# Attention and a two-layer projection on one core: where the second part of batch 0 runs, when w_out is requested, who builds the masks, and which PSUM banks the first projection uses

## The chip, the core and the metric

The kernel runs on one core of a Trainium2 chip. The metric is device time in microseconds (us), the median of several executions of the same program. The profile is of one execution; its span of 255.1 us is a little shorter than the measured time, 256.92 us.

Five engines work side by side, each through its own list of instructions in order: TensorE (PE, matmuls and transposes), VectorE (DVE), ScalarE (ACT), GpSimd (POOL) and SyncE (SP, which here only requests transfers). DMA engines move data between HBM and the core's memory.

## The reference

For 4 batches, 8 heads, 768 positions and 64 numbers per head, attention with one of two masks, then a projection to 2048, a leaky ReLU with a slope per column, and a projection back to 512:

```python
scores = scale * q @ k.T                      # per batch and head, 768 x 768
causal = rel >= 0                             # rel = row - column
stream_keep = causal & (is_sink | in_win)     # first 4 columns, and a window of 64
mask = causal if is_retrieval[h] else stream_keep   # heads 0, 2 and 6 are retrieval heads
a = softmax(where(mask, scores, -1e9))
x = (a @ v), heads side by side               # 3072 tokens x 512
h = x @ w_in                                  # 3072 x 2048
g = maximum(h, 0) + alpha * minimum(h, 0)
out = g @ w_out                               # 3072 x 512, float32
```

## The kernel before

**Segments.** Attention is cut into segments, each of one batch and one pair of heads. Batch 0 is cut in two: segments 0 to 3 ("a") are its first 512 positions, segments 4 to 7 ("b") the other 256. Segments 8 to 19 are batches 1 to 3, whole. A segment runs through pieces: `S` (scores on TensorE, exp on ScalarE, a mask multiplied in on VectorE for segments from 4 on), `AV` (weighted values on TensorE, division on VectorE), and `X` (transposes on TensorE, copy to `xT` on VectorE). `Tq` and `Tk` transpose q and k of the next segment; from segment 12 on a transfer transposes them instead.

**Projections.** Tokens are cut into eight tiles: tile 2b is the first 512 positions of batch b, tile 2b+1 its other 256. `P1(t, f)` computes 128 of the 2048 columns of the first projection for tile t: four matmuls into one PSUM bank, then `neg` (ScalarE, L489) and `g` (VectorE, L490), which frees the bank. `P2(t, s, quarter)` is a quarter, four matmuls, of the second projection for 128 tokens; after four quarters ScalarE copies the result out and a transfer writes it.

**Order of the work.** The order is written out by hand and kept as written (`manual_schedule`). `pieces` lists the attention of segments 4 to 19 in order; `plan` lists units of P1 and P2 to be put between them, spread evenly by cost (a P2 quarter or a 512-wide P1 unit counts 1, a 256-wide P1 unit 0.5). Each entry of `plan` holds the units that run until the last segment of a batch (or of batch 0's second part) is nearly finished; what is left is put there at once, and the next entry begins. After the last piece comes the tail, projections only.

**Before the woven part.** After segments 0 to 3, P1 of tile 0 runs alone for `f` 0 to 12: first three of the four matmuls of units 0 to 4 (the lead), X(3), their fourth matmuls, then units 5 to 12 on up to eight banks. Between these units VectorE builds the multiplicative masks `mr`, `ms` and `ms5` from the additive ones `nmr` and `nms`. Only then do segments 4 to 7 begin, with P1 units 13 to 15 and the first eight units of P2(0) between their pieces.

**Buffers and queues.** Loaded float32 q, k and v rest in `qf`, `kf` and `vf`, four of each in turn. Casts to bf16 are `cast` on GpSimd for segments 0 to 7 (L178 to L199) and `whole_q`, `whole_k`, `whole_v` on VectorE for segments 8 to 19 (L205, L214 or L218, L228), called one or two segments ahead: `whole_q(9)` comes before the first piece of segment 8, `whole_k(9)` before its third, `whole_v(9)` before its fifth. With segment 8 the fifth piece is X(7), the last of batch 0. Loads of q, k and v are requested on SyncE (queue q1 in the profile); `w_in` (three transfers) and `w_out` (four) on GpSimd (q0)[...]. `w_out` is requested right behind `w_in` and the casts of segment 3, ahead of the loads of segments 4 to 11. The memsets of `vf`, `kf`, `kT` and `natk` on GpSimd stand between.

**PSUM.** Of eight banks, `sc0` and `sc1` hold scores, `m0` to `m2` transposes and `AV` results (from segment 4 on `m0` and `m1` only), `mm2` and `m2` P2 results, and P1 takes `mm0` and `mm1`, or the first `wide` names of

```python
WIDE = ["mm0", "mm1", "sc0", "sc1", "mm2", "m0", "m1", "m2"]
```

Of the kernel before, what the change touches and what calls it, by code (L numbers as in the profile page):

```python
# [9 lines left out]
ALU = mybir.AluOpType  # L10
# [4 lines left out]
def kernel(  # L15
# [13 lines left out]
    nc = tc.nc  # L29
    B, H, S, D = q.shape  # L30
# [4 lines left out]
    fp32 = DT.float32  # L35
# [4 lines left out]
    NSINK = 4  # L40
# [5 lines left out]
    CROSS = 12  # L46
# [31 lines left out]
    NSEG = len(SEGS)  # L78
# [5 lines left out]
    ps = ctx.enter_context(tc.tile_pool(name="ps", bufs=1, space=bass.MemoryType.PSUM))  # L84
# [3 lines left out]
    NF, NK, NV, NR, NS = 4, 5, 6, 2, 3  # L88
    qf = [stat.tile([128, 2, 6, 64], fp32, name=f"qf{i}") for i in range(NF)]
    kf = [stat.tile([128, 7, 2, 64], fp32, name=f"kf{i}") for i in range(NF)]  # L90
    vf = [stat.tile([128, 7, 2, 64], fp32, name=f"vf{i}") for i in range(NF)]
# [4 lines left out]
    kT_all = stat.tile([128, NK, 2, 7 * 128], bf16, name="kT")  # L96
# [9 lines left out]
    NATK = [stat.tile([128, 2 * 960], bf16, name=f"natk{i}") for i in range(2)]  # L106
# [14 lines left out]
    def load(n):  # L121
        load_qk(n, nc.sync)
        load_rows(n, v, vf)
# [25 lines left out]
    def ka(n):  # L149
        T = (SEGS[n].q1 - SEGS[n].q0) // 128  # L150
        flat = kf[n % NF].rearrange("p i h d -> p (i h d)")
        return flat[:, 0:2 * T * 64].rearrange("p (h i d) -> p h i d", h=2, d=64)
# [14 lines left out]
    natq, natk = {}, {}  # L167
# [34 lines left out]
    def whole_q(n):  # L202
        sg = SEGS[n]
        nat = natq[n] = NATQ[n % 2]
        nc.vector.tensor_copy(nat.rearrange("p i (h d) -> p h i d", h=2), qf[n % NF])  # L205
        if n >= CROSS:
            nc.sync.dma_start(qT[sg.seq % NK][:, 0:S].rearrange("p (i r) -> p i r", r=128),
                              nat.rearrange("p i c -> p (i c)"), transpose=True)

    def whole_k(n):  # L210
        sg = SEGS[n]
        if n < CROSS:
            natk[n] = NATK1[n % 2]
            nc.vector.tensor_copy(natk[n].rearrange("p i (h d) -> p h i d", h=2), ka(n))  # L214
            return
        flat = NATK[n % 2]
        rows = flat.rearrange("p (h x) -> p h x", h=2)[:, :, 0:896].rearrange("p h (t c) -> p h t c", c=128)
        nc.vector.tensor_copy(rows[:, :, :, 0:D], kf[n % NF].rearrange("p t h d -> p h t d"))  # L218
        sinks(n, rows)
        for hh, h in enumerate(sg.heads):  # L220
            nt = 6 if RETR[h] else 7
            nc.sync.dma_start(kTs[sg.seq % NK][hh][:, 0:128 * nt].rearrange("p (i r) -> p i r", r=128),
                              flat[:, 896 * hh:896 * hh + 128 * nt], transpose=True)

    def whole_v(n):
        sg = SEGS[n]
        vv = vb[sg.seq % NV]
        nc.vector.tensor_copy(vv[:, :, :, 0:D], vf[n % NF])  # L228
        sinks(n, vv.rearrange("p t h c -> p h t c"))

    load_qk(0, nc.scalar)
# [15 lines left out]
    mr = const.tile([128, 5, 144], bf16, name="mr")  # L247
    ms = const.tile([128, 2, 192], bf16, name="ms")
    ms5 = const.tile([128, 2, 192], bf16, name="ms5")
    nmr = const.tile([128, 5, 144], bf16, name="nmr")  # L250
    nms = const.tile([128, 192], bf16, name="nms")
# [35 lines left out]
    def load_w_out(n):  # L287
        nc.gpsimd.dma_start(w_out_b[:, 4 * n:4 * n + 4, :],
                            moe_w_out[512 * n:512 * (n + 1), :].rearrange("(a p) f -> p a f", p=128))
# [175 lines left out]
    TOK = [(b * S + o, w) for b in range(B) for o, w in ((0, SPLIT), (SPLIT, S - SPLIT))]  # L465
    n_mm = [0]


    WIDE = ["mm0", "mm1", "sc0", "sc1", "mm2", "m0", "m1", "m2"]

    def mm_bank(wide=0):
        n_mm[0] += 1
        return ps.tile([128, 512], fp32, tag=WIDE[n_mm[0] % (wide or 2)], name="mm")

    half_done = {}

    def P1(t, f, cs=range(4), wide=0):
        o, w = TOK[t]
        o %= 2 * S
        psg = half_done.pop((t, f)) if (t, f) in half_done else mm_bank(wide)  # L480
        for c in cs:
            a = PAIRS[c][0] // 2
            nc.tensor.matmul(psg[:, 0:w], w_in_b[:, a, 128 * f:128 * (f + 1)], xT[:, c, o:o + w],  # L483
                             start=(c == 0), stop=(c == 3))
        if cs[-1] < 3:
            half_done[t, f] = psg
            return
        neg = work.tile([128, 512], fp32, tag="neg", name="neg", bufs=3)
        nc.scalar.activation(neg[:, 0:w], psg[:, 0:w], AF.Relu, scale=-1.0)  # L489
        nc.vector.scalar_tensor_tensor(g_buf[t % 2][:, f, 0:w], neg[:, 0:w], oma[:, f:f + 1], psg[:, 0:w],  # L490
                                       op0=ALU.mult, op1=ALU.add)
# [16 lines left out]

            (nc.gpsimd if t < 6 else nc.sync).dma_start(out[r:r + 128, :], ot)  # L509

    def p1_units(t, fs=range(16), wide=0):
        return [(TOK[t][1] / 512, lambda f=f: P1(t, f, wide=wide)) for f in fs]

    def p2_units(t):
        return [(1, lambda s=s, u=u: P2(t, s, u)) for s in range(TOK[t][1] // 128) for u in range(4)]
# [33 lines left out]
    for lo, hi in ((0, 512), (512, 1024), (1024, 2048)):  # L549
        load_w_in(lo, hi)  # L550
    cast_v(3)
    for i in range(4):
        load_w_out(i)
    for i in range(NF):
        nc.gpsimd.memset(vf[i][:, 6, :, :], 0.0)
        nc.gpsimd.memset(kf[i][:, 6, :, :], 0.0)
    nc.gpsimd.memset(kT_all[:, 4].bitcast(fp32), 0.0)
    for nat in NATK:
        nc.gpsimd.memset(nat.bitcast(fp32), 0.0)
    for n in range(4, 8):  # L560
        load(n)
        cast(n)
    for n in range(8, 8 + NF):
        load(n)
    for n in range(4):
        sa, sb = seg_scores(n)
        first = [lambda: AV(n - 1, 1)] if n else []
        if n < 3:
            first += [lambda: Tq(n + 1), lambda: Tk(n + 1)]
        seq = sa[:2] + first + sa[2:] + sb[:1]  # L570
        seq += ([lambda: X(n - 1)] if n else []) + sb[1:] + [lambda: AV(n, 0)]
        for piece in seq:
            piece()
        if n == 2:

            tra = ps.tile([128, 16], fp32, tag=misc_tag(), name="tra")
            nc.tensor.transpose(tra, alpha_r, ident_f)
            nc.vector.tensor_scalar(oma, tra, -1.0, 1.0, op0=ALU.mult, op1=ALU.add)
    AV(3, 1)
    LEAD = 5  # L580
    n_misc[1] = 2
    n_mm[0] = -1
    for f in range(LEAD):
        P1(0, f, range(3), wide=5)
    X(3)
    for f in range(LEAD):
        P1(0, f, range(3, 4))
    n_mm[0] = 4
    for f in range(LEAD, 8):
        P1(0, f, wide=8)  # L590
    n_mm[0] = -1
    for f in range(8, 13):
        P1(0, f, wide=5)
        if f == 8:
            nc.vector.tensor_scalar(mr, nmr, 0.0, None, op0=ALU.is_equal)
        elif f < 11:
            nc.vector.tensor_scalar(ms[:, f - 9, :], nms, 0.0, None, op0=ALU.is_equal)
        elif f == 11:

            nc.vector.tensor_copy(ms5[:, 0, :], ms[:, 0, :])  # L600
            nc.vector.tensor_copy(ms5[:, 1, 0:148], ms[:, 0, 0:148])
        else:
            nc.vector.tensor_copy(ms5[:, 1, 148:192], ms[:, 0, 0:44])
            nc.vector.memset(ms5[0:NSINK, 1, 148:152], 0.0)


    pieces = [([], lambda: Tq(4), []), ([], lambda: Tk(4), [])]
    for n in range(4, NSEG):
        seq, x_at = seg_pieces(n)
        for i, piece in enumerate(seq):  # L610
            pre = []
            if i in (0, 2, 4):
                fn = (whole_q, whole_k, whole_v)[i // 2]
                pre = [lambda m=m, fn=fn: fn(m) for m, lo, hi in ((n + 1, 8, CROSS), (n + 2, CROSS, NSEG)) if lo <= m < hi]
            if i == 4 and 8 <= n < NSEG - NF:
                pre.append(lambda n=n: load(n + NF))
            ready = []
            if x_at and i == x_at - 1 and (n - 1) % 4 == 3:
                b = (n - 1) // 4 - 1
                ready = [1] if b == 0 else [2 * b, 2 * b + 1]  # L620
            pieces.append((pre, piece, ready))
# [4 lines left out]
    def merge(a, z):  # L626

        keyed = [((i + 0.5) / len(x), n, u) for n, x in enumerate((a, z)) for i, u in enumerate(x)]
        return [u for _, _, u in sorted(keyed, key=lambda k: k[:2])]


    second = [p2_units(t) for t in range(8)]
    plan = [p1_units(0, range(13, 16)) + second[0][:8],
            merge(second[0][8:], p1_units(1)) + second[1][:6],
            second[1][6:] + p1_units(2) + merge(second[2], p1_units(3)) + second[3][:6],
            second[3][6:] + p1_units(4) + merge(second[4], p1_units(5)) + second[5][:6]]
    units, budget = plan.pop(0), 0
    for i, (pre, piece, ready) in enumerate(pieces):
        for f in pre:
# [9 lines left out]
        while units and budget >= units[0][0] / 2:  # L649
            c, u = units.pop(0)  # L650
            budget -= c
            u()
    n_mm[0] = -1
    for _, u in second[5][6:] + p1_units(6, wide=4) + merge(second[6], p1_units(7, wide=4)) + second[7]:
        u()
    return nc

# [34 lines left out]
```

## Time and profile before

| what | value |
|---|---|
| time, median of 3 runs | 256.92 us (256.82 to 257.19) |
| span of the profiled run | 255.1 us |
| busy: PE, DVE, ACT, POOL | 236.5, 176.3, 143.7, 46.7 us |
| P1 matmuls (L483) | 512, 100.3 us busy |
| P2 matmuls (L502) | 384, 96.9 us busy |
| `neg` (L489), `g` (L490) | 128 each; 491 and 612 ns mean |
| read from HBM, written to HBM | 27.46 MB, 6.29 MB |

The stages on the profile's clock: segments 0 to 3 until about 20.3 us; P1(0) alone until 33.4; segments 4 to 7 until about 58; batch 1 until 97; batch 2 until 153.8; batch 3 until 209.8; the tail until 251.4, after which the last results are written out. A busy time counts an instruction from its start to its end, and neighbouring instructions on one engine overlap by some tens of ns, so sums of durations run a little over the wall time.

### The profile page before, as it was taken

To read this page: it belongs to the slowest core of one execution; us is meant where nothing else is said; L and a number is where in the kernel's file an instruction comes from. 1 tells how busy PE (TensorE), PEld (TensorE's weight loads), DVE (VectorE), ACT (ScalarE), POOL (GpSimd) and SP (SyncE) were. 2 spreads that over 40 slices of the span, in tenths; PEclk is the share of its full clock that TensorE was granted. 3 is DMA by queue.
4 is the path that set the end of the run, shared out by engine and by line. 5 is a ranking of instruction groups with operands and counts; after the bars stand their busy time and mean duration, and the time that the engine had idled before them with its cause. 6 is when DMAs were issued, how large, how long until landed. Compare 5 with 4: busy or idle time off the path is not lost.

```text
span 255.1 us, 5559 instructions
## 1 busy us (share of the span) xinstructions
PE 236.5 (93%) x2079; PEld 145.2 (57%) x2079; DVE 176.3 (69%) x454; ACT 143.7 (56%) x308; POOL 46.7 (18%) x112
## 2 busy tenths in 40 slices
PE   7898988788889999989999999989999999999994
PEld 6784454546676665445666655446666654456651
DVE  6783998786989995897767755887556537853320
ACT  5871884546676556675555537666555426743320
POOL 7899223101012121010111120010000000000000
PEclk9999999999999999999999999999999999999999
DMA  7999999999995999989395992050111111002112
GB/s 213 281 167 210 206 208 234 213 234 229 205 250 104 243 181 240 208 132 191 83 222 136 177 215 88 8 99 1 44 41 41 44 41 44 0 0 84 44 42 82
DMA packets 94563, 34.96 MB, mean 137 GB/s; under 512 B 84920, under 2 KB 92104, under 8 KB 94536
## 3 DMA queue, kind: packets, MB, share of 16 engines
q1 hardware_dynamic: 88824, 25.16, 50.9%
q0 software_dynamic: 5136, 8.91, 14.9%
q10 hardware_dynamic: 576, 0.53, 0.6%
q8 instruction: 16, 0.26, 0.5%
q14 instruction: 11, 0.09, 0.1%
HBM read 27.46 MB, written 6.29 MB: 132 GB/s over the span
## 4 chain that ended last, share of the span: by engine, by line
PE 61%; DVE 16%; DMA 11%; ACT 5%; issue 3%; POOL 1%; SPq 1%; ACTq 0%; DVEq 0%
PE po L502 28%; PE mm L483 22%; DVE g L490 6%; DMA w_in_b<-in_moe_w_in_dram 5%; PE pav L445 4%; ACT neg L489 3%; PE sc L382 2%; DMA vf<-in_v_dram 2%; DMA kf<-in_k_dram 2%; PE sc L414 2%; DMA qf<-in_q_dram 2%; PE tr L460 2%; DVE xn L452 2%; DVE eS L426 1%; DVE kT L327 1%
## 5 line engine op out<-in xcount | busy, mean ns | idle before, releaser
L483 PE MATMUL mm<-xT,w_in_b 128*128 128x512 bf16 (+1 forms) x512 | 100.3, 326 | 4.8 <-DVE g L490 3.0
L490 DVE SCALAR_TENSOR_TENSOR g<-neg,oma,mm 128x512 bf16<-128x512 f32 (+1 forms) x128 | 77.7, 612 | 36.2 <-ACT neg L489 33.6
L502 PE MATMUL po<-w_out_b,g 128*128 128x512 bf16 x384 | 96.9, 379 | 0.0
L489 ACT ACTIVATE neg<-mm 128x512 f32<-128x512 f32 (+1 forms) x128 | 62.5, 491 | 50.5 <-PE mm L483 49.6
L483 PEld LDWEIGHTS <-w_in_b 128*128 128x128 bf16 x512 | 47.9, 97 | 39.4 <-issue 7.0
L502 PEld LDWEIGHTS <-g 128*128 128x128 bf16 x384 | 35.5, 97 | 27.2
L389 ACT ACTIVATE eR<-sc 128x455 bf16<-128x455 f32 (+5 forms) x72 | 38.6, 553 | 16.1 <-PE sc L382 14.6
L421 ACT ACTIVATE eS<-sc 128x384 bf16<-128x384 f32 x60 | 29.2, 490 | 15.5 <-PE sc L414 13.3
L382 PE MATMUL sc<-qT,kT 128*128 128x268 bf16 (+16 forms) x141 | 24.9, 263 | 1.5 <-DVE kT L336 0.8
L506 ACT COPY ot<-po 128x512 f32<-128x512 f32 x24 | 14.0, 585 | 19.7 <-PE po L502 19.7
L509 POOL DMA_DIRECT2D out_dram<-ot x18 | 9.8, 543 | 83.8 <-ACT ot L506 72.5
L426 DVE TENSOR_TENSOR eS<-eS,ms 128x384 bf16<-128x384 bf16 x50 | 17.9, 360 | 7.2 <-ACT eS L421 7.0
L452 DVE TENSOR_TENSOR xn<-pav,rcp 128x448 bf16<-128x448 f32 (+2 forms) x40 | 21.8, 545 | 1.4
L414 PE MATMUL sc<-qT,kT 128*128 128x192 bf16 (+4 forms) x150 | 21.1, 231 | 0.4 <-ACT eR L389 0.3
L392 DVE TENSOR_TENSOR eR<-eR,mr 128x128 bf16<-128x128 bf16 (+4 forms) x60 | 12.8, 232 | 10.7 <-ACT eR L389 10.4
L382 PEld LDWEIGHTS <-kT 128*128 128x128 bf16 x141 | 11.9, 97 | 10.8 <-DVE kT L336 1.9
L414 PEld LDWEIGHTS <-kT 128*128 128x128 bf16 x150 | 13.6, 98 | 5.7
L445 PE MATMUL pav<-vb,eS 128*128 128x65 bf16 x270 | 13.4, 194 | 3.5 <-DVE eS L426 1.9
L445 PEld LDWEIGHTS <-eS 128*128 128x128 bf16 x270 | 11.3, 97 | 7.9 <-DVE eS L426 2.5
L445 PEld LDWEIGHTS <-eR 128*128 128x128 bf16 x336 | 11.8, 97 | 2.5
L462 DVE COPY xT<-tr 128x768 bf16<-128x768 bf16 (+2 forms) x20 | 9.5, 473 | 5.2 <-PE tr L460 5.2
L445 PE MATMUL pav<-vb,eR 128*128 128x65 bf16 x336 | 12.7, 193 | 0.0
(78 smaller groups left out, 154.4 us busy)
## 6 DMA issues: line engine op xcount, KB each, us to landing
qf<-in_q_dram SPq DMA_DIRECT2D x12, 384.0 KB
vf<-in_v_dram SPq DMA_DIRECT2D x24, 192.0 KB
out_dram<-ot POOLq DMA_DIRECT2D x18, 256.0 KB, 3.4
kf<-in_k_dram SPq DMA_DIRECT2D x16, 192.0 KB
w_out_b<-in_moe_w_out_dram POOLq DMA_DIRECT2D x4, 512.0 KB, 18.5
kf<-in_k_dram SPq DMA_DIRECT2D x4, 384.0 KB
out_dram<-ot SPq DMA_DIRECT2D x6, 256.0 KB
qf<-in_q_dram SPq DMA_DIRECT2D x4, 256.0 KB
```

What stands on the lines that cost most here:

```text
L382: nc.tensor.matmul(sc[:, a - lo:z - lo], kt[:, 128 * j:128 * (j + 1)], qt[:, c:c + z - a], start=True, stop=not masked)
L389: nc.scalar.activation(e[:, lo:hi], sc[:, 0:hi - lo], AF.Exp, scale=scale)
L414: nc.tensor.matmul(sc[:, o:o + z - a], kt[:, 128 * j:128 * (j + 1)], qt[:, 124 * j + a:124 * j + z], start=True, stop=not on_pe)
L421: nc.scalar.activation(two, sc[:, 0:384].rearrange("p (s c) -> p s c", c=192), AF.Exp, scale=scale)
L426: nc.vector.tensor_tensor(two, two, ms5 if first == 4 else ms, op=ALU.mult)
L445: nc.tensor.matmul(pav[:, i, :], e[:, o:o + 128], vv[:, j, hh, 0:D + 1], start=(m == 0), stop=(m == len(terms) - 1))
L452: nc.vector.tensor_tensor(xn[n][:, lo:hi, 64 * hh:64 * hh + 64], pav[:, lo:hi, 0:D], rcp[:, lo:hi].to_broadcast([128, hi - lo, D]), op=ALU ...
L483: nc.tensor.matmul(psg[:, 0:w], w_in_b[:, a, 128 * f:128 * (f + 1)], xT[:, c, o:o + w], start=(c == 0), stop=(c == 3))
L489: nc.scalar.activation(neg[:, 0:w], psg[:, 0:w], AF.Relu, scale=-1.0)
L490: nc.vector.scalar_tensor_tensor(g_buf[t % 2][:, f, 0:w], neg[:, 0:w], oma[:, f:f + 1], psg[:, 0:w], op0=ALU.mult, op1=ALU.add)
L502: nc.tensor.matmul(po[t], g_buf[t % 2][:, f, 128 * s:128 * (s + 1)], w_out_b[:, f, :], start=(f == 0), stop=(f == 15))
L506: nc.scalar.copy(ot, po.pop(t))
```

## The change

The first projection of tile 0 no longer runs alone. After its lead of five units, segments 4 to 7 begin at once, and units 5 to 15 are put between their pieces, on four banks (`mm0`, `mm1`, `mm2`, `m2`), which are free for them because no P2 unit runs there any more. All of P2(0) moves behind X(7), into batch 1, and the later entries of the plan are shifted to suit: P1 of an even tile is now merged with the rest of the P2 before it, not put behind it. In the tail, P2(5) is merged with P1(6).

To let segments 4 to 8 start early, their loads go ahead of `w_out`, which GpSimd now requests behind its casts of q and k of segment 8. Those casts, and that of v, move from VectorE to GpSimd; the casts of q of segments 9 to 11 move to ScalarE. The masks are built on GpSimd, before the loads of segments 4 to 7 come in, since segment 4 needs them earlier and VectorE is busy then.

```diff
-        nc.vector.tensor_copy(nat.rearrange("p i (h d) -> p h i d", h=2), qf[n % NF])
+        copy = nc.gpsimd.tensor_copy if n == 8 else nc.scalar.copy if n < CROSS else nc.vector.tensor_copy
+        copy(nat.rearrange("p i (h d) -> p h i d", h=2), qf[n % NF])
...
-            nc.vector.tensor_copy(natk[n].rearrange("p i (h d) -> p h i d", h=2), ka(n))
+            (nc.gpsimd if n == 8 else nc.vector).tensor_copy(natk[n].rearrange("p i (h d) -> p h i d", h=2), ka(n))
...
-        nc.vector.tensor_copy(vv[:, :, :, 0:D], vf[n % NF])
+        (nc.gpsimd if n == 8 else nc.vector).tensor_copy(vv[:, :, :, 0:D], vf[n % NF])
...
+    BANKS = {"beside P2": ["mm0", "mm1"], "beside attention": ["mm0", "mm1", "mm2", "m2"],
+             "lead": ["mm0", "mm1", "sc0", "sc1", "mm2"], "tail": ["mm0", "mm1", "sc0", "sc1"]}
...
     cast_v(3)
-    for i in range(4):
-        load_w_out(i)
+
+    nc.gpsimd.tensor_scalar(mr, nmr, 0.0, None, op0=ALU.is_equal)
+    for i in range(2):
+        nc.gpsimd.tensor_scalar(ms[:, i, :], nms, 0.0, None, op0=ALU.is_equal)
+    nc.gpsimd.tensor_copy(ms5[:, 0, :], ms[:, 0, :])
+    nc.gpsimd.tensor_copy(ms5[:, 1, 0:148], ms[:, 0, 0:148])
+    nc.gpsimd.tensor_copy(ms5[:, 1, 148:192], ms[:, 0, 0:44])
+    nc.gpsimd.memset(ms5[0:NSINK, 1, 148:152], 0.0)
     for i in range(NF):
         nc.gpsimd.memset(vf[i][:, 6, :, :], 0.0)
-        nc.gpsimd.memset(kf[i][:, 6, :, :], 0.0)
-    nc.gpsimd.memset(kT_all[:, 4].bitcast(fp32), 0.0)
-    for nat in NATK:
-        nc.gpsimd.memset(nat.bitcast(fp32), 0.0)
     for n in range(4, 8):
         load(n)
         cast(n)
-    for n in range(8, 8 + NF):
+    for i in range(NF):
+        nc.gpsimd.memset(kf[i][:, 6, :, :], 0.0)
+    nc.gpsimd.memset(kT_all[:, 4].bitcast(fp32), 0.0)
+    load(8)
+    whole_q(8)
+    whole_k(8)
+    for i in range(4):
+        load_w_out(i)
+    whole_v(8)
+    for n in range(9, 8 + NF):
         load(n)
+    for nat in NATK:
+        nc.gpsimd.memset(nat.bitcast(fp32), 0.0)
...
-    n_mm[0] = 4
-    for f in range(LEAD, 8):
-        P1(0, f, wide=8)
     n_mm[0] = -1
-    for f in range(8, 13):
-        P1(0, f, wide=5)
-        if f == 8:
-            nc.vector.tensor_scalar(mr, nmr, 0.0, None, op0=ALU.is_equal)
...
-    plan = [p1_units(0, range(13, 16)) + second[0][:8],
-            merge(second[0][8:], p1_units(1)) + second[1][:6],
-            second[1][6:] + p1_units(2) + merge(second[2], p1_units(3)) + second[3][:6],
-            second[3][6:] + p1_units(4) + merge(second[4], p1_units(5)) + second[5][:6]]
+    hidden = [p1_units(t) for t in range(6)]
+    plan = [p1_units(0, range(LEAD, 16), "beside attention"),
+            hidden[1][:6] + merge(second[0], hidden[1][6:]) + second[1][:4],
+            merge(second[1][4:], hidden[2]) + merge(second[2], hidden[3]) + second[3][:2],
+            merge(second[3][2:], hidden[4]) + merge(second[4], hidden[5]) + second[5][:2]]
...
-    for _, u in second[5][6:] + p1_units(6, wide=4) + merge(second[6], p1_units(7, wide=4)) + second[7]:
+    for _, u in merge(second[5][2:], p1_units(6, where="tail")) + merge(second[6], p1_units(7, where="tail")) + second[7]:
         u()
```

More of the change, by code (lines that the diff above doesn't have):

```diff
@@ L466, with mm_bank, P1 @@
     n_mm = [0]
-    WIDE = ["mm0", "mm1", "sc0", "sc1", "mm2", "m0", "m1", "m2"]
-    def mm_bank(wide=0):
+    BANKS = {"beside P2": ["mm0", "mm1"], "beside attention": ["mm0", "mm1", "mm2", "m2"],
+             "lead": ["mm0", "mm1", "sc0", "sc1", "mm2"], "tail": ["mm0", "mm1", "sc0", "sc1"]}
+    def mm_bank(where):
         n_mm[0] += 1
-        return ps.tile([128, 512], fp32, tag=WIDE[n_mm[0] % (wide or 2)], name="mm")
+        return ps.tile([128, 512], fp32, tag=BANKS[where][n_mm[0] % len(BANKS[where])], name="mm")
     half_done = {}
-    def P1(t, f, cs=range(4), wide=0):
+    def P1(t, f, cs=range(4), where="beside P2"):
         o, w = TOK[t]
         o %= 2 * S
-        psg = half_done.pop((t, f)) if (t, f) in half_done else mm_bank(wide)
+        psg = half_done.pop((t, f)) if (t, f) in half_done else mm_bank(where)
         for c in cs:
@@ L509, in P2, with p1_units @@
             (nc.gpsimd if t < 6 else nc.sync).dma_start(out[r:r + 128, :], ot)
-    def p1_units(t, fs=range(16), wide=0):
-        return [(TOK[t][1] / 512, lambda f=f: P1(t, f, wide=wide)) for f in fs]
+    def p1_units(t, fs=range(16), where="beside P2"):
+        return [(TOK[t][1] / 512, lambda f=f: P1(t, f, where=where)) for f in fs]
     def p2_units(t):
@@ L583 @@
     for f in range(LEAD):
-        P1(0, f, range(3), wide=5)
+        P1(0, f, range(3), where="lead")
     X(3)
@@ L587 @@
         P1(0, f, range(3, 4))
-    n_mm[0] = 4
-    for f in range(LEAD, 8):
-        P1(0, f, wide=8)
     n_mm[0] = -1
-    for f in range(8, 13):
-        P1(0, f, wide=5)
-        if f == 8:
-            nc.vector.tensor_scalar(mr, nmr, 0.0, None, op0=ALU.is_equal)
[L596 to L604, printed above, removed]
     pieces = [([], lambda: Tq(4), []), ([], lambda: Tk(4), [])]
@@ L613 @@
                 fn = (whole_q, whole_k, whole_v)[i // 2]
-                pre = [lambda m=m, fn=fn: fn(m) for m, lo, hi in ((n + 1, 8, CROSS), (n + 2, CROSS, NSEG)) if lo <= m < hi]
+                pre = [lambda m=m, fn=fn: fn(m) for m, lo, hi in ((n + 1, 9, CROSS), (n + 2, CROSS, NSEG)) if lo <= m < hi]
             if i == 4 and 8 <= n < NSEG - NF:
```

## The prediction

> **What bounds the kernel now.** I read the page's engine shares first: TensorE is busy in 93% of the span, yet a busy share cannot say whether it is running or waiting inside a pipeline. So I took the start of every matmul from TensorE's timeline and gave each the spacing it has where nothing stands in front: 0.216 us for 512 columns (64 in 13.81 us in the chain of waits below), in proportion for fewer, 0.030 us for 65 columns (27 in 0.81 us), 0.056 us for a transpose (six from 52.63 to 52.97). Wall minus this work is stall. The stages come from the windows view (start:end, length, busy us of each engine, clock, DMA share, GB/s):
>
> ```profile
> 20.30:33.40 13.10, 12.19 (x65) 5.42 (x64) 8.91 (x17) 6.84 (x12) 6.86 (x21) 1.00 1.18 208
> 33.40:58.40 25.00, 19.99 (x217) 12.20 (x215) 21.34 (x77) 14.52 (x33) 5.24 (x16) 1.00 1.14 221
> 58.40:97.20 38.80, 36.67 (x408) 25.84 (x408) 33.30 (x99) 24.62 (x57) 5.57 (x13) 1.00 1.00 205
> 97.20:119.00 21.80, 20.14 (x164) 10.63 (x163) 17.37 (x37) 15.05 (x29) 1.79 (x5) 1.00 1.12 188
> 119.00:153.80 34.80, 34.80 (x305) 22.25 (x303) 23.76 (x61) 18.13 (x43) 5.01 (x11) 1.00 0.87 170
> 153.80:175.00 21.20, 19.59 (x139) 10.02 (x137) 16.58 (x36) 14.82 (x29) 1.79 (x5) 1.00 0.22 49
> 175.00:209.80 34.80, 34.70 (x323) 22.31 (x321) 19.46 (x50) 16.14 (x39) 2.70 (x5) 1.00 0.10 39
> 209.80:251.40 41.60, 41.52 (x225) 21.71 (x222) 19.64 (x32) 18.85 (x39) 0.54 (x1) 1.00 0.10 39
> ```
>
> Stall by my count, stage by stage: 1.6 (first projection alone), 7.4 (second part of batch 0), 4.2 (batch 1), 3.3 (P1 of tile 2 beside batch 2), 0.5, 3.3 (P1 of tile 4 beside batch 3), 0.8, 0.65 (tail). TensorE's work is the same in both kernels, so only these 22 us can be won, and any delay adds. After 58.4 us they sum to 12.8.
>
> In the two 3.3 us stages the chain of waits (start, length, what) shows why: with two banks, P1 waits for ScalarE's `neg`, then VectorE's `g`, 2.4 us per two units.
>
> ```profile
> 102.26 0.61 ACT neg L489
> 102.86 0.03 issue
> 102.89 0.76 DVE g L490
> 103.65 0.04 issue
> 103.69 1.04 PE mm L483 x4
> ...
> 209.81 13.81 PE mm L483 x64
> ```
>
> From 20 to 58 us the DMA engines are full as well. The DMA view of 25 to 40 us (queue: packets, MB, share) shows the weights' queue q0 taking three times what q1, with q, k and v, gets; meanwhile GpSimd's timeline shows casts of segment 5 waiting for loads:
>
> ```profile
> q0 software_dynamic: 2122, 2.30, 88.8%
> q1 hardware_dynamic: 2118, 0.79, 30.7%
> ...
> 28.77 0.40 POOL L178 CAST g<-qf 128x256 bf16<-128x256 f32 x1 [2.46 <-DMA qf<-in_q_dram]
> 30.66 0.40 POOL L178 CAST g<-kf 128x256 bf16<-128x256 f32 x1 [1.50 <-DMA kf<-in_k_dram]
> ```
>
> The end of batch 0 is this stretch of VectorE's timeline; the last row is what the first P1 of tile 1 waits for:
>
> ```profile
> 56.97 0.55 DVE L214 CAST natm<-kf 128x768 bf16<-128x768 f32 x1
> ...
> 57.57 0.62 DVE L228 CAST vb<-vf 128x896 bf16<-128x896 f32 x1
> 58.10 0.28 DVE L462 COPY xT<-tr 128x256 bf16<-128x256 bf16 x1
> ```
>
> `whole_k(9)` and `whole_v(9)` stand ahead of it in VectorE's order, in both kernels. Adding up q1's packets in order of end puts q, k and v of segment 9 at about 49, 51 and 53 us: four to six us of slack, no more.
>
> [...]
>
> **The change part by part.**
> *P1(0) units 5 to 12 leave the stage 20.3:33.4* and go beside segments 4 to 7. The lead (20 matmuls, 4.3 us, with X(3)'s wait) ends at about 25.3, so `Tq(4)` comes some 8 us sooner. Those segments keep eleven filler units (before 3 of P1 and 8 of P2; now 11 of P1). Each P1 in place of a P2 adds 0.6 us ScalarE and about 0.67 us VectorE (0.75 less the overlap with its neighbour): 8 x 0.67 = 5.4 us more on VectorE.
> *Four banks* for these units: they remove a wait that would otherwise be the 2.4 us per two units above; price nothing.
> *Masks to GpSimd*: VectorE loses seven small operations, 1.3 us (0.34, 2 x 0.20, 0.20, 0.19, 0.17, 0.06). On GpSimd, unseen before: between these 1.3 us and about 2.3 us by its `nmr` and `nms` rows (0.81 for 720 columns, 0.35 for 192); I take 2.3. It replaces the 3.0 us of `w_out` issues in front of the `vf` memsets that hold the queue of loads until 21.1 us, so nothing is lost.
> *Casts of segment 8 to GpSimd*: VectorE loses 0.55 + 0.55 + 0.62 less overlaps, 1.5 us. GpSimd's price, from 0.61 us at 512 columns: 0.91 each for q and k, 1.07 for v. Hidden behind segments 6 and 7. *q of 9 to 11 to ScalarE*: 0.47 us each off VectorE, near 0.8 us on ScalarE (its 768-column `qT` copy); the one for 9 now holds back the exps of segment 8 until q has landed.
> *`w_out` later.* `w_in` lands at 28.9 as before; then q1 alone has some 204 GB/s. Segments 5 to 7 (about 0.9 MB left) are in by 33.5, q and k of 8 by 37.5, GpSimd's casts done by 38.5; behind them `w_out` is requested, 2.1 MB as written. Alternating packets then give it about 160 GB/s for 13 us, to 52, and segment 9 the rest: its v lands last. The bytes ahead of it are those of before (53 us), so I put it at 55, bounds 53 and 57. P2(0) starts after that; `w_out` itself delays nothing.
> So segments 4 to 7, whose own pace would be 25.3 + 21 (before) + 5.4 - 1.5 - 0.5 = 49 to 50, run into the wait for k and v of 9 in VectorE's order: xT is copied near 56.1, not 58.1. That is **2.0 us won**, while eight P2 units, 8 x 0.863 = **6.9 us of work, are left over**.
> *Batch 1* must take 28 units instead of 22 (a half-width P1 counted as half). A P2 unit (0.86 us) where a half P1 (0.43) stood covers five waits of about 0.5 us before AV by 0.4 each: 4.2 becomes 2.2.
> *Batches 2 and 3*: P1(2) and P1(4) get four P2 units in between instead of two in front. Each absorbs about 0.45 us of bank wait: 3.3 becomes 1.3 to 1.5, I take 1.3, twice; the rest stays at 0.5 each.
> *Tail*: four P2 units more, in a stage without stalls; work only moves. The later merge and its own four banks: nothing.
> Stall after the xT copy: 2.2 + 1.3 + 0.5 + 1.3 + 0.5 + 0.65 = 6.4 instead of 12.8. **Sum: -2.0 + 6.9 - 6.4 = -1.5 us, 255.4 us.**
>
> **Rivals.**
> *Slower: loads and VectorE take the gain back.* Segment 9 lands at 56 (xT 1 us sooner) and the weave saves only 3.3 of the 12.8, because VectorE is busy 33.3 of 38.8 us in batch 1 and the P2 units stand at the wrong joints: -1.0 + 6.9 - 3.3 = +2.6, 259.5 us. For it: the DMA row at 1.14 to 1.18 in both stages. Against: the fast stage 119:153.8, where P2 alternates with P1.
> *Much faster: segment 9 isn't held.* [...]segment 9 comes first; segments 4 to 7 set their own pace, xT is copied at 52.7 (-5.4), and the weave brings stall down to 5.0 (-7.8): -5.4 + 6.9 - 7.8 = -6.3, 250.6 us.[...]
>
> **How the numbers follow.** Main case 0.50, slower rival 0.28, faster rival 0.22. Predicted is the main case, 255.4. Faster than 256.4: the faster rival, and three quarters of the main case (its terms are good to about 1.5 us): 0.22 + 0.38 = 0.60. Within 0.2%: 0.12, from the main case's edge. Slower: 0.28. The range takes in most of both rivals and the bounds of segment 9's landing: 250.8 to 259.2.
>
> **What would show it.** `w_out` issues on GpSimd near 38 to 42 us; `whole_k(9)` and `whole_v(9)` on VectorE waiting for DMA at 52 to 55; xT at 56; TensorE idle just before; no gaps before P1 in the two former 3.3 us stages. It is wrong if VectorE never waits there (faster), or if gaps in batch 1 grow (slower).

## The result and the profile after

| | before | after |
|---|---|---|
| time, median | 257.06 us (256.82 to 257.82) | 260.56 us (259.2 to 261.31) |
| ratio after to before | | 1.0125, 95% interval 1.0077 to 1.0173 |
| span of the profiled execution | 255.1 us | 257.4 us |
| mean granted TensorE clock | 0.998 | 0.986 |

The change makes the kernel 3.5 us slower; 255.4 was predicted. The profiled execution of after is the fastest of its four (259.2 us), so the traces account for 2.3 us. All four executions show clocks of 0.984 to 0.986; what lifts the other three by another 1.2 to 2.1 us was not settled.

The windows view of after, with the columns and nearly the stages of before:

```profile
20.30:33.40 13.10, 10.72 (x81) 5.41 (x80) 8.58 (x21) 6.85 (x15) 7.54 (x27) 1.00 0.90 188
33.40:58.40 25.00, 16.99 (x168) 10.38 (x169) 19.43 (x61) 13.61 (x30) 10.11 (x19) 0.93 1.20 203
58.40:97.20 38.80, 38.18 (x407) 26.55 (x406) 31.15 (x92) 25.53 (x56) 4.82 (x11) 0.96 1.02 200
97.20:119.00 21.80, 21.36 (x174) 11.62 (x173) 17.53 (x40) 15.49 (x30) 2.52 (x7) 1.00 1.04 202
...
153.80:175.00 21.20, 20.29 (x171) 11.07 (x168) 16.10 (x36) 13.64 (x27) 1.79 (x5) 1.00 0.40 68
```

Two things are to be seen. In the stage 33.4:58.4 TensorE is busy 16.99 us against 19.99, in the same 25 us. And the clock column, 1.00 everywhere before, reads 0.93 and 0.96 in two stages. With the prediction's own count (wall minus matmul work), the three terms of its sum came out so:

| term | predicted | measured |
|---|---|---|
| copy of `xT` by X(7), the end of batch 0 | 2.0 us sooner | 0.2 us sooner (57.87 against 58.10) |
| P2 units left over | +6.9 | +6.8 |
| stall after that copy | 12.8 to 6.4 | 12.8 to 8.5 |
| sum | -1.5 | +2.3 |

VectorE's timeline shows the end of batch 0 (start, length, what; in brackets the idle time before it and what ended it):

```profile
55.61 0.55 DVE L215 CAST natm<-kf 128x768 bf16<-128x768 f32 x1
...
57.33 0.63 DVE L229 CAST vb<-vf 128x896 bf16<-128x896 f32 x1 [0.37 <-DMA vf<-in_v_dram]
57.87 0.28 DVE L463 COPY xT<-tr 128x256 bf16<-128x256 bf16 x1
```

VectorE reaches `whole_v(9)` at 56.96 and waits 0.37 us for its load; for `whole_k(9)` it never waits. Such a small wait looks harmless. It isn't: two bounds end here nearly together, a late VectorE and a late load, and taking away either shows only the other. The chain of waits shows the load (start, length, what):

```profile
43.88 13.23 DMA vf<-in_v_dram
...
57.33 0.63 DVE vb L229
57.95 0.21 DVE xT L463
```

The DMA view of 42 to 57.2 us shows who had the engines meanwhile. Queue q0 is `w_out`, q1 all of q, k and v:

```profile
q0 software_dynamic: 2018, 2.00, 78.9%
q1 hardware_dynamic: 4353, 1.10, 42.7%
```

The same view of 46 to 54 us, where both queues have work all the time, shows as many packets on each, but those of q1 a quarter as large:

```profile
q0 software_dynamic: 1250, 1.25, 91.7%
q1 hardware_dynamic: 1249, 0.32, 29.8%
```

SyncE's timeline adds that its two requests of v of segment 9 themselves took 8.26 us here, against 2.40 in the run late_w below, where `w_out` comes later. From 41 to 44 us q1 moved only 0.03 MB, though they had begun. Why is not settled. The two rows, after and late_w:

```profile
40.46 8.26 SPq L162 DMA_DIRECT2D vf<-in_v_dram  x2
```

```profile
40.77 2.40 SPq L162 DMA_DIRECT2D vf<-in_v_dram  x2
```

And TensorE's timeline shows both thin stretches and what follows them:

```profile
46.37 0.36 PE L446 MATMUL pav<-vb,eS 128*128 128x65 bf16 x6 [0.78 <-DVE eS L429]
48.48 0.45 PE L461 MATMUL tr<-ident,xn 128*128 128x128 bf16 x3 [1.75 <-DVE xn L453]
48.73 1.91 PE L485 MATMUL mm<-xT,w_in_b 128*128 128x512 bf16 x4
...
58.20 0.27 PE L485 MATMUL mm<-xT,w_in_b 128*128 128x256 bf16 x1 [1.78 <-DVE xT L463]
```

Four matmuls of 512 columns, 1.02 us elsewhere, take 1.91 at 48.73: the clock is halved (0.50 from 48.57 to 51.99, see The clock).

### The profile page after: what moved, and what is told of

The parts are those of the page before. It is cut to its first block, busy times and chain, and to the rows that moved or that the text cites. A ratio compares the mean times of both kernels' runs of the same rounds, so it can differ in the third digit from the quotient of the medians.

```text
span 257.4 us, 5550 instructions
## 1 busy us (share of the span) xinstructions
PE 237.1 (92%) x2079; PEld 146.2 (57%) x2079; DVE 173.8 (68%) x441; ACT 145.8 (57%) x311; POOL 53.0 (21%) x122
## 4 chain that ended last, share of the span: by engine, by line
PE 70%; DMA 14%; POOL 6%; DVE 3%; ACT 2%; issue 1%; SPq 1%; ACTq 0%; DVEq 0%; POOLq 0%
PE po L504 32%; PE mm L485 25%; DMA vf<-in_v_dram 10%; PE pav L446 5%; PE sc L383 3%; PE sc L415 3%; DMA qf<-in_q_dram 2%; PE tr L461 2%; DVE g L492 2%; DMA kf<-in_k_dram 2%; ACT neg L491 1%; DVE xn L453 1%; PE tr L302 1%; POOL w_in_b L286 1%; POOL mr L555 1%
## 5 line engine op out<-in xcount | busy, mean ns | idle before, releaser
L485 PE MATMUL mm<-xT,w_in_b 128*128 128x512 bf16 (+1 forms) x512 | 104.5, 330 | 4.2 <-DVE xT L463 2.3
L504 PEld LDWEIGHTS <-g 128*128 128x128 bf16 x384 | 35.4, 97 | 28.6
L383 PE MATMUL sc<-qT,kT 128*128 128x268 bf16 (+16 forms) x141 | 26.0, 267 | 1.8 <-DVE kT L337 0.8
L383 PEld LDWEIGHTS <-kT 128*128 128x128 bf16 x141 | 12.3, 99 | 13.7 <-issue 2.9
L393 DVE TENSOR_TENSOR eR<-eR,mr 128x128 bf16<-128x128 bf16 (+4 forms) x60 | 13.7, 244 | 8.7 <-ACT eR L390 8.5
L415 PEld LDWEIGHTS <-kT 128*128 128x128 bf16 x150 | 13.9, 98 | 6.7
L446 PE MATMUL pav<-vb,eS 128*128 128x65 bf16 x270 | 12.3, 193 | 2.3 <-DVE eS L429 2.0
L461 PE MATMUL tr<-ident,xn 128*128 128x128 bf16 x116 | 9.9, 221 | 4.7 <-DVE xn L453 4.6
```

The costliest lines, as they stand in the source:

```text
L383: nc.tensor.matmul(sc[:, a - lo:z - lo], kt[:, 128 * j:128 * (j + 1)], qt[:, c:c + z - a], start=True, stop=not masked)
L415: nc.tensor.matmul(sc[:, o:o + z - a], kt[:, 128 * j:128 * (j + 1)], qt[:, 124 * j + a:124 * j + z], start=True, stop=not on_pe)
L446: nc.tensor.matmul(pav[:, i, :], e[:, o:o + 128], vv[:, j, hh, 0:D + 1], start=(m == 0), stop=(m == len(terms) - 1))
L461: nc.tensor.transpose(tr[:, QS[i]:QS[i] + 128], nat[:, i, :], ident)
L504: nc.tensor.matmul(po[t], g_buf[t % 2][:, f, 128 * s:128 * (s + 1)], w_out_b[:, f, :], start=(f == 0), stop=(f == 15))
```

## The experiments

In all of them one number is compared beside the time: the way from the first matmul of P1(0) to the copy of `xT` by X(7), since the traces' clocks lie up to 1.5 us apart. It is 37.8 us before and 37.5 after (predicted 35.7). Each is one trace's; weave (below) is the kernel before in this stretch and shows 37.3, so differences of half a us say nothing. The median of before was 256.92 to 257.01 beside every experiment.

| kernel | time, us | ratio to before | first P1(0) to xT of X(7), us |
|---|---|---|---|
| after | 260.56 | 1.0077 to 1.0173 | 37.5 |
| late_w | 257.38 | 0.9993 to 1.0022 | 35.5 |
| reorder9 | 257.04 | 0.9974 to 1.0006 | 35.4 |
| early_w | 262.24 | 1.0156 to 1.0238 | 40.0 |
| no_g | 261.03 | 1.0124 to 1.0195 | 38.3 |
| late_w_no_g | 256.98 | 0.9988 to 1.0011 | 34.6 |
| late_w_no_g2 | 255.01 | 0.9907 to 0.9948 | 32.4 |
| warm | 259.32 | 1.0056 to 1.0118 | 37.2 |
| engines | 259.87 | 1.0061 to 1.0133 | 40.2 |
| reorder9_dve8 | 258.02 | 1.0019 to 1.0045 | 36.5 |
| reorder9_masks | 257.28 | 0.9990 to 1.0018 | 34.8 |
| weave | 256.50 | 0.9970 to 0.9993 | 37.3 |
| weave_reorder9 | 256.00 | 0.9953 to 0.9996 | 37.0 |

### Is it segment 9's load, and VectorE's order behind it?

**late_w**: GpSimd requests `w_out` only when v of segment 9 is there.

```diff
-    for i in range(4):
-        load_w_out(i)
     whole_v(8)
     for n in range(9, 8 + NF):
         load(n)
+    seen = const.tile([128, 7, 2, 1], fp32, name="seen")
+    nc.gpsimd.tensor_copy(seen, vf[9 % NF][:, :, :, 0:1])
+    for i in range(4):
+        load_w_out(i)
```

> The changed kernel, but GpSimd requests w_out only once segment 9's v has landed (a small GpSimd copy of vf reads it first), and casts v of segment 8 before that. Theory L (the late landing of segment 9 holds back the end of batch 0): v of 9 lands near 45 us instead of 57, xT of segment 7 is copied 3 us or more before 57.9, time 3 us or more under the changed kernel's 260.6. Theory P (segments 4 to 7 are slow by themselves, because neg and g of eleven P1 units stand in ScalarE's and VectorE's order between their own steps): VectorE reaches whole_v(9) at 57.0 anyway, so xT moves by less than 1 us and the time by less than 1.5 us. Under both, P2(0) starts later than w_out's landing or just at it (60 us).

**reorder9**: the loads stay as in after, but VectorE casts k and v of segment 9 behind X(7).

```diff
+                if n == 8 and i:
+                    pre = []
+            if n == 8 and i in (6, 8):
+                pre = [lambda i=i: (whole_k, whole_v)[i // 2 - 3](9)]
```

> The changed kernel with whole_k(9) and whole_v(9) called before the seventh and ninth pieces of segment 8 instead of the third and fifth, so that X(7) and its copy no longer stand behind them on VectorE; w_out stays where it is. If only VectorE's order makes the late landing of segment 9 count: xT at 55.5 to 56, no wait for DMA ahead of it, time 2 to 3.5 us under 260.6 (w_out behind segment 9 won 3.2). If the wait only moves on to Tk(9): xT at 56, but less than 1 us won.

**early_w**: the opposite, `load_w_out` right behind `load_w_in`, ahead of the masks.

> The changed kernel with w_out requested where it was before, right behind w_in and ahead of the masks. By before's trace segments 5, 6 and 7 then land at 33, 40 and 45 us, and 9 at 53 to 54 instead of 57. If the later request of w_out is what holds segment 9 back: xT of segment 7 at 56 to 56.5 as with w_out behind segment 9, time 2 to 3.5 us under 260.6. If the earlier loads of segments 5 to 7 are what matters to the woven part: their Tq and Tk wait for casts, xT at 58 or later, time 260 or more.

Either cure alone brings the copy of `xT` 2.0 to 2.1 us sooner and the time back by more than 3 us, to that of before. The copy of late_w lies between what its two theories said (3 us or more, less than 1): the late load counts, and it is not all. VectorE's timeline of late_w shows the copy without a wait ahead of it:

```profile
55.71 0.62 DVE L229 CAST vb<-vf 128x896 bf16<-128x896 f32 x1
56.24 0.29 DVE L463 COPY xT<-tr 128x256 bf16<-128x256 bf16 x1
```

VectorE's timeline of reorder9 shows the casts behind the copy, where nothing of TensorE waits for them; the loads come exactly as in after:

```profile
56.93 0.28 DVE L463 COPY xT<-tr 128x256 bf16<-128x256 bf16 x1
...
59.10 0.55 DVE L215 CAST natm<-kf 128x768 bf16<-128x768 f32 x1
...
61.01 0.62 DVE L229 CAST vb<-vf 128x896 bf16<-128x896 f32 x1
```

So `w_out`'s bytes do harm only through that place in VectorE's order. early_w shows that in after's order a request ahead of the masks brings the copy 2.5 us later (the intervals of the two times overlap a little). It mixes two delays: GpSimd's `vf` memsets, which release the loads of segments 4 to 7, now stand behind `w_out` and the masks and run at 24.80 instead of 22.05, and then the loads come in beside `w_out`, as in before, where from 25 to 40 us the weights' q0 moved 2.30 MB and q1 0.79. GpSimd casts k of segment 5 at 33.85, after 1.47 us of waiting for it (29.31 in after), and q of segment 6 at 38.58 (30.43): some 3 us of this is GpSimd's order (24.80 against 22.05); the rest, 1.8 and 5.4 us, is put down to the sharing as an estimate.

### What sets VectorE's own pace?

**no_g**, **late_w_no_g** and **late_w_no_g2** leave out `neg` and `g` of P1(0)'s woven units, alone and with late_w. GpSimd sets that part of the buffer `g` to zero instead, so the result is not the reference's; the third does this earlier.

```diff
+        if t == 0 and f >= 5:
+            return
         neg = work.tile([128, 512], fp32, tag="neg", name="neg", bufs=3)
```

> The changed kernel without neg and g of units 5 to 15 of P1 of tile 0 (left out; g's place is filled by one GpSimd memset behind the casts of segment 8, so that P2 reads zeros there). The matmuls stay. Theory P: segments 4 to 7 go at the pace that they had beside P2 (21 us), VectorE reaches whole_v(9) near 50 us, where it then waits for v of segment 9 until 57: xT at 57.5 to 58, time less than 1.5 us under the changed kernel, but with a wait for DMA of 5 us or more on VectorE. Theory L alone: as the changed kernel, with no such wait.

> Both edits: w_out requested behind segment 9, and neg and g of units 5 to 15 of P1 of tile 0 left out (zeros in their place). If both hold (two bounds that end at the same time): xT near 50 to 52 us, and the time 5 to 7 us under the changed kernel. If one alone counted, no better than the better of the two single runs by more than 1 us.

> As the run with w_out behind segment 9 and neg and g of units 5 to 15 of P1(0) left out (zeros in their place), but the GpSimd memset that stands in for them comes before GpSimd's wait for segment 9, not between w_out and the end of the part: in the run before, VectorE's cast of k of 9 took 5.5 us while GpSimd wrote w_out's requests and that memset. If that overlap alone kept xT at 55.3: the cast takes 0.55 to 3.5 us and xT comes at 50 to 53, time 2 us or more under the 257.0 of that run. If the part has another bound: xT at 55 again.

In no_g the copy of X(6) comes 3.5 us sooner than in after (45.43 against 48.97), and nothing is won: VectorE's timeline shows the time turned into waiting for segment 9. (Its second wait is put down to q; the cast reads v, and q, k and v of a segment are requested one behind the other on q1, in after at 37.46, 37.92 and 40.46 us.)

```profile
54.74 0.56 DVE L215 CAST natm<-kf 128x768 bf16<-128x768 f32 x1 [3.35 <-DMA kf<-in_k_dram]
...
58.19 0.63 DVE L229 CAST vb<-vf 128x896 bf16<-128x896 f32 x1 [2.75 <-DMA qf<-in_q_dram]
58.73 0.28 DVE L463 COPY xT<-tr 128x256 bf16<-128x256 bf16 x1
```

With the load out of the way too (late_w_no_g2) the copy comes 5.2 us sooner than in after. That shows two bounds: 2.0 us for one cure (late_w), nothing for the other (no_g), 5.2 for both. What the second bound is made of is shown only in part: `neg` on ScalarE and `g` on VectorE were left out together. In after, VectorE is busy 19.43 of the 25 us from 33.4 to 58.4 and waits 4.6 us for `neg` between 25 and 58, so it is its order, with the waits in it, that sets the pace; ScalarE's part was not taken apart.

late_w_no_g won less, for a reason that I hadn't foreseen. Its VectorE cast of k of segment 9 took 5.52 us instead of 0.55, beside a GpSimd without a pause:

```profile
49.24 5.52 DVE L215 CAST natm<-kf 128x768 bf16<-128x768 f32 x1
```

```profile
47.16 3.06 POOL L289 DMA_DIRECT2D w_out_b<-in_moe_w_out_dram  x4 [0.25 <-issue]
50.16 2.50 POOL L583 MEMSET g<- 128x2816 f32 x1
52.54 1.80 POOL L585 MEMSET natk<- 128x960 f32 x2
```

With the `g` memset moved out of that row (late_w_no_g2) the same cast took 2.99 us. In both it ended 0.4 us after GpSimd's row did (54.76 and 54.34; 52.34 and 51.92). So the cast lasted until GpSimd's row was over, several instructions long; what held it was not shown.

### Casts and masks on GpSimd

**engines**: before, with the casts of segment 8 on GpSimd and those of q of 9 to 11 on ScalarE, nothing else.

> The kernel before with only the casts moved: q, k and v of segment 8 on GpSimd, q of 9 to 11 on ScalarE, at their old places in the order; masks, w_out, P1(0) and the plan as before. VectorE loses 3.0 us in segments 7 to 10. If VectorE's order bounds the end of batch 0: xT of segment 7 up to 1 us sooner, time 0.3 to 1 us under before (257.0). If GpSimd's casts shut VectorE out meanwhile (a mask multiply took 1.28 us instead of 0.38 beside one), or ScalarE's copies hold back the exps: no change or slower by up to 1 us.

It costs 2.9 us, more than was expected. GpSimd, which in before's order comes to the casts late, runs the three back to back, and VectorE's multiply by the mask takes 2.51 us beside them. GpSimd, VectorE and TensorE of this kernel:

```profile
50.05 0.84 POOL L206 CAST natq<-qf 128x768 bf16<-128x768 f32 x1
50.81 0.84 POOL L215 CAST natm<-kf 128x768 bf16<-128x768 f32 x1
51.59 0.94 POOL L229 CAST vb<-vf 128x896 bf16<-128x896 f32 x1
```

```profile
50.23 2.51 DVE L427 TENSOR_TENSOR eS<-eS,ms 128x384 bf16<-128x384 bf16 x1
```

```profile
53.05 0.35 PE L446 MATMUL pav<-vb,eS 128*128 128x65 bf16 x6 [2.26 <-DVE eS L429]
```

The multiply takes 0.36 us when GpSimd is idle (at 45.49 in the same trace), so this makes up some 2.1 us. The rest was not taken apart: all four executions have a halved clock for a while (below), and ScalarE's copy of q of segment 9 was moved in the same run. In after the same casts lie apart, at 36.61, 38.41 and 42.20, and only beside the third was VectorE seen to lose time: two `eR` multiplies took 1.28 us instead of 0.38, 0.9 us more.

**reorder9_dve8** asks what the move is worth there: reorder9 with the three casts back on VectorE, and `w_out` requested once v of segment 8 has landed (at 41.81 in its trace, 39.05 in reorder9's).

> reorder9 (after, with k and v of segment 9 cast behind X(7)) and, besides, q, k and v of segment 8 cast on VectorE among the pieces of segment 7, as in before; GpSimd requests w_out once v of segment 8 has landed (a small copy from it stands ahead). Theory 'GpSimd's casts cost VectorE their own time[...]': the three casts cost VectorE 1.5 us, but the eR multiplies at 42 us lose the 1.8 us that they took beside GpSimd's cast of v, and so xT(7) is copied where it was in reorder9 (56.9) or up to half a us sooner; time 256.3 to 257.0. Rival 'the move to GpSimd was worth it': xT(7) comes 1.0 to 1.5 us later than in reorder9 and the time is 257.8 to 258.5.

The rival held: 1.1 us later and 258.02 us. Part of it is the clock (below): among the executions in which the clock was halved for a while, the medians are 258.09 us here and 257.34 in reorder9. So in after's order the casts are better on GpSimd, if the later `w_out` cost nothing here, as it did not in late_w. That VectorE was slow beside GpSimd's casts (2.51 us for 0.36 in engines, 1.28 for 0.38 in after) doesn't condemn the move; its place does.

**reorder9_masks** puts the `vf` memsets, which release the loads of segments 4 to 7, ahead of the mask operations.

> The changed kernel with whole_k(9) and whole_v(9) behind X(7) (257.0), and the memsets of vf ahead of the seven mask operations on GpSimd instead of behind them, so that SyncE's loads go on near 18.5 us and not 22.3. If GpSimd's 4.1 us for the masks cost time through the loads: v of segment 4 is cast sooner than 27.0 us, xT sooner by 0.5 us or more, time 256 to 256.5. If segments 4 to 7 are bound by ScalarE and VectorE: xT and time within 0.5 us of that run.

The masks took GpSimd 4.1 us and not 2.3, and the loads were released 1.3 us later than before (memsets from 22.05 instead of 20.79). GpSimd's timeline of after:

```profile
17.91 2.02 POOL L555 TENSOR_SCALAR mr<-nmr 128x720 bf16<-128x720 bf16 x1
19.92 1.33 POOL L557 TENSOR_SCALAR ms<-nms 128x192 bf16<-128x192 bf16 x2
...
22.05 0.63 POOL L564 MEMSET vf<- 128x128 f32 x4
```

Moving the loads ahead of them gave 0.6 us at X(7) in its trace and nothing in the time that the intervals could tell.

### The clock

**warm** fills the three thin stretches with 60 idle matmuls, whose result is never read (P1 gives up the bank that they write):

```diff
+    def keep(n):
+        idle = ps.tile([128, 512], fp32, tag="m2", name="idle")
+        for i in range(n):
+            nc.tensor.matmul(idle[:, 0:128], ident, ident, start=True, stop=True)
...
+        if n in (5, 6):
+            keep({5: 12, 6: 24}[n])
...
+            if (t, f, c) == (1, 0, 3):
+                keep(24)
```

> The changed kernel with 60 idle matmuls (128 columns, the identity, result never read) where TensorE waits in the batch-0 part: 12 ahead of X(5), 24 ahead of X(6), 24 ahead of the last matmul of the first P1 unit of tile 1; P1 beside attention has three banks instead of four, the fourth takes their results. Theory C (the two stretches of 3.4 us at half clock cost time): granted clock 1.00 in most runs, the time 1.5 to 2.5 us under the changed kernel's 260.6. Rival (they lie in waits that are there anyway): clock 1.00, time within 0.7 us of 260.6. If the idle matmuls delay X, at most 1 us is lost again.

All four executions now have a clock of 0.998 to 0.999, and the median is 1.2 us under after's, though the two intervals overlap. The copy of `xT` is hardly sooner, and VectorE's timeline says why: with the clock kept up, VectorE reaches `whole_v(9)` earlier and waits the rest of the time for the load.

```profile
55.99 0.74 DVE L501 SCALAR_TENSOR_TENSOR g<-neg,oma,mm 128x512 bf16<-128x512 f32 x1
58.17 0.63 DVE L229 CAST vb<-vf 128x896 bf16<-128x896 f32 x1 [1.44 <-DMA qf<-in_q_dram]
58.71 0.28 DVE L470 COPY xT<-tr 128x256 bf16<-128x256 bf16 x1
```

So the 0.37 us of after had been 1.4 us, hidden under a halved clock. The record of the clock gives the two spells of after, 48.57 to 51.99 and 58.81 to 62.23, both 3.41 us and 10.24 us apart from start to start, three times that length. The windows view, cut at it:

```profile
45.16:48.57 3.41, 0.87 (x20) 0.64 (x17) 3.10 (x13) 0.95 (x3) 0.10 (x1) 1.00 1.21 196
48.57:51.99 3.42, 3.42 (x21) 2.29 (x22) 0.98 (x2) 1.27 (x2) 0.00 (x0) 0.50 1.22 196
51.99:55.40 3.41, 2.98 (x28) 1.45 (x26) 3.25 (x13) 3.01 (x8) 0.00 (x0) 1.00 1.21 203
55.40:58.81 3.41, 1.36 (x13) 0.97 (x13) 2.38 (x6) 1.26 (x4) 0.34 (x1) 1.00 1.32 243
58.81:62.23 3.42, 3.42 (x23) 2.60 (x22) 1.86 (x5) 2.81 (x7) 0.00 (x0) 0.50 0.77 161
```

Each halved stretch follows one of the same length in which TensorE did little, though its longest pauses were 1.75 and 1.78 us: by the spacing of its matmuls, 15% and 32% of the stretch were filled. In no_g the longest pause in such a stretch (42.43 to 45.84) was 1.10 us. From the first P1 to the tail, over the fourteen traces, ten such stretches were filled 32% or less, and each was followed by a halved one; none filled 40% or more at full clock was. (An eleventh halved stretch, in late_w_no_g, followed one that was itself at half clock and filled 60%. Several traces lack some matmul records, and no_g shows three of the four matmuls of a P1 unit in its stretch, so a fill can be some points too low.) What sets the clock was not shown. Of one program some executions were halved and others not (10 of 20 in late_w). As an estimate of how often, from these figures alone, I laid stretches of 3.41 us end to end over each trace, one per kernel, at 40 offsets, and counted the offsets at which one is filled less than 36%, a limit between 32 and 40:

| kernel | offsets with a thin stretch (estimate) | executions that were halved |
|---|---|---|
| before | 0 of 40 | 0 of 117 |
| after | 21 of 40 | 4 of 4 |
| reorder9_masks | 17 of 40 | 6 of 12 |
| reorder9 | 23 of 40 | 4 of 12 |
| late_w | 25 of 40 | 10 of 20 |
| late_w_no_g2 | 29 of 40 | 11 of 13 |
| reorder9_dve8 | 31 of 40 | 15 of 17 |
| engines | 35 of 40 | 4 of 4 |
| no_g, late_w_no_g, early_w | 40 of 40 | 20 of 20 |
| weave; weave_reorder9 | 2 of 40 each | 1 of 20; 2 of 13 |
| warm | 0 of 40 | 0 of 4 |

The two columns rise together, though not strictly (reorder9 and reorder9_masks stand the other way round). Three programs with at least four executions on each side give the price of one spell, the same program at full and at halved clock: in late_w the medians are 256.75 and 257.70 us, in reorder9_masks 256.86 and 257.43, in reorder9 257.03 and 257.34, so **0.3 to 1 us for one spell**. After has two, and its second, beside batch 1, shows 0.8 us in the stalls (batch 1 takes 40.5 us from the copy to P1(2), and 39.7 in reorder9).

### The later plan alone

**weave**: before, with P1 of even tiles merged with the P2 before it and the boundaries moved (`second[1][:4]`, `second[3][:2]`, and so on), all else as it was.

> The kernel before with only the later part of the plan changed: P1 of tiles 2 and 4 merged with four quarters of P2 (before two of them in front), four P2 quarters more in the tail, merged there with P1(6); P1(0), w_out, masks and casts as before. By the two profiles the stall beside P1(2) fell from 3.3 to 1.4 us and beside P1(4) from 3.3 to 1.8, so 3.5 us are to be won: 253.5 us. If that gain belonged to what is shifted from batch 1 instead, the time stays within 1 us of before.

It gains 0.5 us, not the 3.5 of the expectation. From the first P1(2) to the first P1(4) it takes 53.2 us where before took 56.6, with two P2 units fewer (1.7 us): 1.7 us won. From there to P1(6) it wins 0.8. But batch 1, which gave those units away, needs 37.1 us instead of 38.6 with four fewer (3.45 us of work): 1.9 us of new stall. P2 units are a fixed stock of filler, and most of what they cover in one place they leave open in another.

### A version from the parts that paid

**weave_reorder9**: before, the later plan, and k and v of segment 9 cast behind X(7); nothing of the early part.

> The kernel before with the later part of the plan changed (that alone gave 256.5) and whole_k(9) and whole_v(9) moved behind X(7). Before, they stand 1.0 us of VectorE time ahead of X(7)'s copy, and TensorE waits 0.8 us for it: 0.5 to 1 us won, 255.5 to 256.0. If TensorE only waits elsewhere: 256.5.

At 256.00 us it has the lowest median of the kernels here that do all the work, 0.04 to 0.47% under before; its interval overlaps that of weave, so what the second move adds is not shown.

## Why the prediction was wrong

The mechanism named in it, `whole_v(9)` waiting in VectorE's order behind `w_out`, was there. Its sizes were not, and one effect was missing. Of the 3.8 us between the predicted -1.5 and the +2.3 of the traces, 1.8 lie ahead of the copy and 2.1 in the stall behind it, of which 0.8 is the clock (0.1 went the other way, in P2); the rest of the difference in time is the 1.4 us by which after's median lies above its profiled execution, and stays open.

*"xT is copied near 56.1".* This step failed: 57.87. Two terms of it were too short.

The load: `w_out` was requested at 39.18 to 42.24, as foreseen (38 to 42), and took the share that was foreseen (1.25 MB in 8 us is 156 GB/s, against 160, an estimate from packets that alternate; the views show as many on each queue, 2122 and 2118 before, 1250 and 1249 after, not their order). But its last part landed at 55.7, not 52: q0 had moved only 0.01 MB by 40.9, and 2.1 MB at that rate take 13 us more, so the end could not come before 54. With it v of segment 9 landed at 57.1, not 55, at the outer bound (57).

The segments' own pace: the prediction counted "49 to 50" to the first scores of segment 8, and the faster rival's 52.7 adds the 3 us from there to the copy. With the load out of the way and full clock, late_w and reorder9 copy `xT` at 55.8 on after's time scale, 3.1 us later. So the rival's 52.7 was never to be had; only leaving out eleven `neg` and `g` brings it there (late_w_no_g2). In after what VectorE lost beside GpSimd's cast (0.9 us at 42.00) and a halved clock come on top. What makes up the 3.1 us was not taken apart.

*P1 in place of P2 on VectorE, 5.4 us.* Right in kind: from `Tq(4)` to the copy of X(6), three of the four segments, it takes 23.0 us after and 18.7 before. Leaving out `neg` and `g` brings it to 19.6, 3.4 us less, ScalarE's `neg` included.

*P2 units left over, 6.9 us.* Right (6.8).

*Stall after the copy, 6.4 us.* Measured 8.5, of which 0.8 is the second halved spell. Without it, reorder9 has 7.7: batch 1 2.3 (predicted 2.2), P1(2) 1.4 (1.3), P1(4) 1.85 (1.3), the plain P1(3) and P1(5) stretches 0.4 and 1.1 (0.5 each), tail 0.6 (0.65). The weave's terms were good to 0.6 us each; 5.1 of the 6.4 us came.

*The clock* was taken as 1.0 throughout. This step was put at nothing without a reason, and cost 0.8 us behind the copy. Taking work out of a stage where TensorE waits for VectorE thinned out TensorE (16.99 us busy in 33.4:58.4 against 19.99), and the prediction held that "any delay adds" without asking about the clock, which was halved behind the stretches that were filled 15 and 32%.

*Masks, 2.3 us:* 4.1, without consequence that could be measured. *Casts of segment 8, "hidden behind segments 6 and 7":* hidden apart from the 0.9 us above.

*The rivals.* "Slower: loads and VectorE take the gain back", 259.5 us, is nearest in kind and time, with other terms: xT 0.2 sooner, not 1.0, and the weave saved 4.3, not 3.3.

So where did the gain go? Even with segment 9 cured, after equals before (reorder9, 0.9974 to 1.0006). Batch 0 ends some 2 us sooner only, since its attention keeps VectorE's pace; the 6.9 us of P2 that left it come back later, and cover only 5.1 us of stall there.

## What to carry to other kernels

Before moving filler out of a stage, ask which engine sets that stage's pace: here TensorE became free and VectorE didn't, so TensorE idled, and the moved work was paid for later. In an in-order queue, put instructions that wait for a transfer behind those that another engine is waiting for; that alone recovered 3.5 us here (in the traces 2.1 at the copy and 0.8 in batch 1, without the second halved spell). And a small wait at a join of two late chains says nothing of what either costs: take away each alone and both together.

## What was not expected of the hardware

- In after, TensorE's clock was halved twice for 3.41 us, behind stretches of that length that were 15 and 32% filled, with no pause over 1.78 us in them; in no_g behind one with no pause over 1.10 us.
- An instruction of VectorE took far longer beside a GpSimd that went on without a pause: 2.51 us for a multiply of 0.36 (engines), 5.52 us for a cast of 0.55 (late_w_no_g).
- GpSimd's comparison of 720 bf16 columns took 2.02 us where VectorE took 0.34, while its cast of 768 columns (0.82) was near VectorE's 0.55.
